# Gated linear attention and a GELU FFN on one core: one early table load, 112-row loads, halved copies in two units, and identity products in TensorE's waits

## The chip, the cores and the metric

The kernel runs on one core of a Trainium2 chip. The metric is the device time of one execution in microseconds. A core has five engines with a queue each, which run their instructions in the order of the program: TensorE (PE, with PEld for its weight loads), VectorE (DVE), ScalarE (ACT), GpSimd (POOL) and SyncE (SP, which here only issues transfers). A wait in one queue holds everything behind it.

## The reference, cut to what matters

```python
state = np.zeros((B, H, D, D))                 # B 4, H 8, S 768, D 48
for t in range(S):
    state = alpha[:, :, t, :, None] * state + np.einsum('bhd,bhe->bhde', k[:, :, t], v[:, :, t])
    y[:, :, t] = np.einsum('bhd,bhde->bhe', q[:, :, t], state)
x = y.transpose(0, 2, 1, 3).reshape(B * S, H * D)     # 3072 x 384
h = x @ w_in                                          # 384 x 2048
g = 0.5 * h * (1.0 + erf(h / sqrt(2)))
out = g @ w_out                                       # 2048 x 384
```

A recurrence with a decay per channel runs over 768 steps; its result is the input of a two-layer network with an exact GELU.

## The kernel before, in words

The sequence is cut into 12 groups g of 256 tokens, and each group into two units u of four heads: unit n = 2g + u. A unit is loaded as three tiles, alpha, keys and queries (`load_data`), two heads on partitions 0 to 47 and 64 to 111. Then VectorE scans alpha forward and backward (`ahead`, L254 and L263) and scales queries (L259) and keys (L268). TensorE makes the scores and turns the keys into one PSUM pair of banks (`scores`, `turned`, L283 and L291). ScalarE copies the turned keys out (kn, L301) and VectorE masks the scores (ss, L306); the two read the same two banks, and the program keeps them apart in time. TensorE makes the part inside a chunk and the states' increments (`inside`, L323 and L340), VectorE chains the states (`chain`, L358 and L360), TensorE adds the part from earlier chunks (`outside_part`, L384). The result is split into a high and a low part (x_high on ScalarE, L435, x_low on VectorE, L439). When both units of a group are there, `spread` (L448) moves 48-row pieces to their place by six small transfers, from the SP and the ACT queue in the first groups. Only then can the FFN of the group start.

The FFN's weights come in 16 pieces of 768 KB (`fetch`, L203, three buffers `st`). Each is turned into a high and a low part in four steps: top (ACT, L218), join (DVE, L222), high (ACT, L232), low (DVE, L235). Then `gemm1` (L456) multiplies x by w_in in three products, ScalarE makes the GELU twice (L522, L523), VectorE the low rest (L528), and `gemm2` (L540) multiplies by w_out. From group 4 on, two groups are taken together (L472, L490).

The order of instructions is set by a planner at build time: a list of operations with an engine, a cost from the table `COST`, the operations they wait for and a rank. It walks through time in steps of 0.05 and, whenever an engine is free, places the ready operation with the lowest rank; TensorE takes FFN steps when nothing of the recurrence is ready. The order that comes out is then written as it is into the engine's queues. A second thing that the planner does not see: each transfer uses one of eight semaphore lanes in turn, and the issue of a transfer waits until the one before on its lane has landed.

At the start 18 products of an identity matrix run on TensorE (L110) while the first data come in. After units 0 and 1 four range checks of alpha per group (`range_check`, L176, two per unit) are placed on ScalarE; the load of the unit that will use the same buffer waits for them.

Of the kernel before, what the change touches and what calls it, by code (L numbers as in the profile page):

```python
# [21 lines left out]
WARM = 18  # L22
# [15 lines left out]
def gla_then_gelu_ffn(ctx: ExitStack, tc: tile.TileContext, q, k, v, alpha, qg, kg, ag, vg, q0, k0, a0, w_in, w_out, out):  # L38
    nc = tc.nc
# [52 lines left out]
    y_first = first.tile([P, 2, BANK], F32, name="yfirst")  # L92
# [4 lines left out]
    def y_of(n):  # L97
        return y_first if n == 1 else ybank if n < SPLIT else sbank
# [203 lines left out]

    def masked(g, u):
        d = cur[g, u]
        d["ss"] = room(NU * g + u).tile([P, 2, NCH, CS], F32, tag="ss", bufs=1, name=f"ss_{g}_{u}")
        nc.vector.tensor_tensor(  # L306
            out=d["ss"],
            in0=d["s"][:, :, : 2 * C].rearrange("p h (c t) -> p h c t", t=CS),
            in1=mask.unsqueeze(1).unsqueeze(1).to_broadcast([P, 2, NCH, CS]),
            op=ALU.mult,  # L310
        )
# [390 lines left out]
    def plan_unit(n):  # L702
# [316 lines left out]
```

## Time and profile before

| what | value |
|---|---|
| median of 3 runs | 520.96 us (520.43 to 521.4) |
| the profiled execution | 520.84 us, of which its span is 519.0 us |
| TensorE busy | 489.8 us, 94% of the span |
| VectorE busy | 251.8 us, 49% |
| ScalarE busy | 200.4 us, 39% |
| moved by all transfers | 40.20 MB |

Times in the rows below are in microseconds from the start of the span unless marked ns. "Idle before" is time in which the engine had nothing to run, with what ended it. PEclk is the clock granted to TensorE as a share of 2.4 GHz: 1.00 is 2.4 GHz, 0.50 is 1.2 GHz.

### The profile page before, as it was taken

What the parts mean: (1) busy time and instruction counts of PE and PEld (TensorE: products, weight loads), DVE (VectorE), ACT (ScalarE), POOL (GpSimd) and SP (SyncE); (2) the same over time, 40 slices, a digit from 0 to 9 for tenths busy, and PEclk for the clock granted to TensorE, in tenths of its full rate; (3) what the DMA queues carried; (4) which work ended last, traced back from release to release, by engine and by line L of the source; (5) the groups of instructions that cost most, each with busy time, mean ns of one, the idle gap of its engine ahead of it and who ended that gap; (6) DMA issues with size and microseconds to landing.
All of it is one profiled execution on the core that took longest, in us unless ns stands there. A gap on an engine that the chain in (4) does not pass through costs nothing.

```text
span 519.0 us, 12171 instructions
## 1 busy us (share of the span) xinstructions
PE 489.8 (94%) x5190; PEld 418.8 (81%) x5190; DVE 251.8 (49%) x486; ACT 200.4 (39%) x386; POOL 31.3 (6%) x42
## 2 busy tenths in 40 slices
PE   5657999999999999999999999999999999999994
PEld 5556889899998999988888777788777788888883
DVE  4879977998888565121111558521433121211212
ACT  1647757445543342222222543232544222231311
POOL 2000001112211111000000101100000000000000
PEclk9569999999999999999999999999999999999998
DMA  8587757325541421000000332300100000100001
GB/s 317 176 268 230 239 145 231 92 58 159 139 129 43 140 80 46 1 30 1 1 1 1 107 92 56 85 1 0 63 18 3 14 1 0 62 0 1 0 1 67
DMA packets 24542, 40.20 MB, mean 77 GB/s; under 512 B 3872, under 2 KB 11616, under 8 KB 24480
## 3 DMA queue, kind: packets, MB, share of 16 engines
q1 hardware_dynamic: 22736, 34.06, 22.0%
q0 software_dynamic: 880, 3.93, 2.0%
q10 hardware_dynamic: 864, 1.34, 0.8%
q8 instruction: 43, 0.70, 0.6%
q14 instruction: 19, 0.16, 0.1%
HBM read 32.24 MB, written 4.72 MB: 71 GB/s over the span
## 4 chain that ended last, share of the span: by engine, by line
PE 82%; DVE 7%; ACT 4%; DMA 4%; issue 1%; SPq 0%; ACTq 0%; DVEq 0%
PE hw L472 26%; PE accw L490 17%; PE acc L540 10%; PE hp L456 9%; PE ybank L490 8%; DMA st<-in_moe_w_in_dram 2%; PE sbank L283 2%; PE sbank L291 2%; PE sbank L323 1%; PE sbank L384 1%; DMA ad<-in_ag_dram 1%; DVE st L222 1%; DVE pp L254 1%; ACT top L218 1%; PE ybank L323 1%
## 5 line engine op out<-in xcount | busy, mean ns | idle before, releaser
L528 DVE TENSOR_TENSOR glo<-hw,ghi 128x512 fp32r<-128x512 f32 x64 | 44.2, 691 | 172.3 <-ACT hw L523 172.3
L472 PE MATMUL hw<-x,wih 128*128 128x512 f32 x384 | 121.9, 398 | 0.0
L522 ACT ACTIVATE ghi<-hw 128x512 fp32r<-128x512 f32 x64 | 38.3, 598 | 177.7 <-PE hw L472 177.7
L472 PEld LDWEIGHTS hw<-x,wih 128*128 128x128 f32 x384 | 71.0, 188 | 16.1
L456 PE MATMUL hp<-x,wih 128*128 128x256 f32 x384 | 73.5, 291 | 7.6 <-DMA x<-z 7.5
L472 PE MATMUL hw<-x,wil 128*128 128x512 f32 x192 | 75.9, 395 | 0.0
L456 PEld LDWEIGHTS hp<-x,wih 128*128 128x128 f32 x384 | 60.9, 194 | 9.0 <-ACT top L218 7.7
L456 PE MATMUL hp<-x,wil 128*128 128x256 f32 x192 | 54.8, 286 | 0.0
L490 PE MATMUL accw<-ghi,woh 128*128 128x512 f32 x128 | 51.1, 399 | 0.0
L490 PE MATMUL accw<-ghi,wol 128*128 128x512 f32 x128 | 50.2, 393 | 0.0
L540 PE MATMUL acc<-woh,ghi 128*128 128x384 f32 x128 | 44.9, 351 | 0.0
L472 PEld LDWEIGHTS hw<-x,wil 128*128 128x128 f32 x192 | 36.0, 188 | 9.0
L540 PE MATMUL acc<-wol,ghi 128*128 128x384 f32 x128 | 43.0, 336 | 0.0
L490 PE MATMUL accw<-glo,woh 128*128 128x512 f32 x128 | 40.3, 391 | 0.0
L522 ACT ACTIVATE ghi<-hp 128x512 fp32r<-128x512 f32 x32 | 19.1, 598 | 52.3 <-PE hp L456 51.3
L523 ACT ACTIVATE hw<-hw 128x512 f32<-128x512 f32 x64 | 37.9, 592 | 0.0
L456 PEld LDWEIGHTS hp<-x,wil 128*128 128x128 f32 x192 | 37.3, 194 | 0.0
L263 DVE TENSOR_TENSOR_SCAN rp<-ad,rp,top 128x255 f32<-128x255 f32 x48 | 36.8, 809 | 0.1
L259 POOL TENSOR_TENSOR qd<-qd,pp 128x512 f32<-128x512 f32 x18 | 23.5, 1308 | 200.6 <-DMA st<-in_moe_w_in_dram 81.6
L528 DVE TENSOR_TENSOR glo<-hp,ghi 128x512 fp32r<-128x512 f32 x32 | 22.0, 686 | 22.3 <-ACT hp L523 22.1
L254 DVE TENSOR_TENSOR_SCAN pp<-ad,top 128x256 f32<-128x256 f32 x48 | 30.4, 675 | 4.9 <-DMA ad<-in_a_dram 4.9
L306 DVE TENSOR_TENSOR ss<-sbank,mask 128x512 f32<-128x512 f32 x23 | 15.9, 690 | 29.3 <-ACT kn L301 29.1
(105 smaller groups left out, 695.3 us busy)
## 6 DMA issues: line engine op xcount, KB each, us to landing
st<-in_moe_w_in_dram SPq DMA_DIRECT2D x8, 768.0 KB, 5.8
st<-in_moe_w_out_dram SPq DMA_DIRECT2D x8, 768.0 KB, 5.8
vn<-in_vg_dram SPq DMA_DIRECT2D x12, 384.0 KB, 5.1
ad<-in_ag_dram SPq DMA_DIRECT2D x40, 96.0 KB, 3.0
kd<-in_kg_dram SPq DMA_DIRECT2D x40, 96.0 KB, 2.3
qd<-in_qg_dram SPq DMA_DIRECT2D x40, 96.0 KB, 2.7
out_dram<-parts POOLq DMA_DIRECT2D x3, 768.0 KB, 3.6
x<-z SPq DMA_DIRECT2D x63, 32.0 KB, 2.0
```

Source lines behind the costliest of these rows:

```text
L254: nc.vector.tensor_tensor_scan(pp[:, i], at[:, i], top, MID, ALU.mult, ALU.min)
L259: (nc.vector if g < NSB else nc.gpsimd).tensor_tensor(out=qt, in0=qt, in1=pp, op=ALU.mult)
L263: nc.vector.tensor_tensor_scan(rp[:, i, G - 2 :: -1], at[:, i, G - 1 : 0 : -1], top[:, 1:], rp[:, i, G - 1 :], ALU.mult, ALU.min)
L283: nc.tensor.matmul(d["s"][o, h, t], lhsT=d["kt"][r, (2 * j + i) * CS : (2 * j + i + 1) * CS], rhs=d["qt"][r, i, t], start=True, stop=True)
L306: nc.vector.tensor_tensor(out=d["ss"], in0=d["s"][:, :, : 2 * C].rearrange("p h (c t) -> p h c t", t=CS), in1=mask.unsqueeze(1).unsqueeze( ...
L456: nc.tensor.matmul(hp[:, j, :], lhsT=a[:, j, i * P : (i + 1) * P], rhs=x[:, i, :], start=(i == 0 and n == 0), stop=(i == NK - 1 and n == 2),)
L472: nc.tensor.matmul(h, lhsT=a[:, j, i * P : (i + 1) * P], rhs=x[:, i, part], start=(i == 0 and n == 0), stop=(i == NK - 1 and n == 2),)
L490: nc.tensor.matmul(acc[i], lhsT=w[:, j, e], rhs=a, start=(f == 0 and k == 0 and w is wo_hi[f2]), stop=(f == NF - 1 and k == 1),)
L522: nc.scalar.activation(ghi, hp, AF.Gelu)
L523: nc.scalar.activation(hp, hp, AF.Gelu)
L528: nc.vector.tensor_tensor(out=glo, in0=hp, in1=ghi.bitcast(F32), op=ALU.subtract)
L540: nc.tensor.matmul(acc[t], lhsT=a[:, j, t * C : (t + 1) * C], rhs=w[:, j, :], start=(first and j == 0 and k == 0 and w is wo_hi[f]), stop= ...
```

## The change

ScalarE loads the table of the GELU as its first instruction (`preload_act_table`), ahead of its three transfer issues; the program then has one table load where it had two. All units are laid out with 64 rows for the first head, so that a load is one transfer of 112 rows (units 4 on) or 128 rows (the first four) where it was two of 48. In units 0 and 1 the copy of the keys and the mask are cut in two, one bank each, in opposite order. Unit 1 writes its result into `sbank` in place of a pair of banks of its own; that pair is now `spare_bank`, the target of the identity products, which nothing reads. Their number at the start is 22 where it was 18, and the planner places one more wherever, after its time 8.0 and before the first FFN step, TensorE has nothing ready for 0.33 (`turn`). The range checks of groups 0 and 1 wait until the spread of group 0 has landed, and the first step of weight pieces 0 and 1 waits for the copy of the keys of unit 0 and 1. Costs of a load and of the spread are set anew.

```diff
-WARM = 18
+WARM = 22
...
     def y_of(n):
-        return y_first if n == 1 else ybank if n < SPLIT else sbank
+        return sbank if n == 1 else ybank if n < SPLIT else sbank
...
-    warm = small_bank([P, P], "warm")
+    nc.scalar.preload_act_table(AF.Gelu)
+    def turn_over():
+        nc.tensor.matmul(spare_bank[:, 0, :P], lhsT=ident, rhs=ident, start=True, stop=True)
+
     for _ in range(WARM):
-        nc.tensor.matmul(warm, lhsT=ident, rhs=ident, start=True, stop=True)
+        turn_over()
...
-            if n < NB * NU:
-                eng = nc.scalar if n < NU and (i + u) % 2 else nc.sync
-                eng.dma_start(to, first[n])
-                continue
-            for h in range(2):
-                nc.sync.dma_start(to[h * DP : h * DP + D], src[g - NB, u, h])
+            rows = slice(0, P if n < NB * NU else DP + D)
+            eng = nc.scalar if n < NU and (i + u) % 2 else nc.sync
+            eng.dma_start(data[g % NB][name][rows, p].rearrange("p a t -> p (a t)"), src[n, rows])
...
-        nc.scalar.copy(d["kn"], d["s"][:, :, 2 * C : 4 * C])
+        for b in (slice(1, 2), slice(0, 1)) if NU * g + u < NU else (slice(0, 2),):
+            nc.scalar.copy(d["kn"][:, b], d["s"][:, b, 2 * C : 4 * C])
...
+        for b in (slice(0, 1), slice(1, 2)) if NU * g + u < NU else (slice(0, 2),):
+            nc.vector.tensor_tensor(
+                out=d["ss"][:, b],
...
+            if g == 1:
+                for o in (unit[u]["c%d" % side], d["c%d" % side]):
+                    o.deps.append(ready_x[0])
         if u == NU - 1:
             ready_x[g] = op("SP", "spread", lambda: spread(g), [d["xl"]], rank=-100, lands=3.2)
-            if g >= NSB:
-                ready_x[g].cost *= 2
+            ready_x[g].cost *= 2 if g >= NSB else 0.8
...
+    for n in range(NU):
+        wops[n]["u"].deps.append(unit[n]["kn"])
...
+        if 8.0 < t and not steps:
+            soon = [at for o in waiting["PE"] for at in [when(o)] if at is not None]
+            if not soon or min(soon) > t + COST["turn"]:
+                return Op("PE", "turn", turn_over)
```

What this makes of the queues is shown at three places. The first is TensorE from its start to the first FFN step; `hp_0` is the first FFN product, `sbank`, `sfirst`, `ybank` and `yfirst` are pairs of banks, `spare` is the pair that nobody reads. Before:

```order
L110 MATMUL sbank<-ident 128x128 x18
L283 MATMUL sbank<-qd_112,kd_111 64x64 x16
L291 MATMUL sbank<-ident,kd_111 128x128 x4
L323 MATMUL ybank<-ss_0_237,vn_109 64x64 x16
L340 MATMUL ybank<-vn_109,kn_0_235 64x48 x16
L283 MATMUL sfirst<-qd_112,kd_111 64x64 x16
L291 MATMUL sfirst<-ident,kd_111 128x128 x4
L384 MATMUL ybank<-qd_112,state_1_120 48x64 x4
...
L323 MATMUL yfirst<-ss_1_314,vn_109 64x64 x16
L340 MATMUL yfirst<-vn_109,kn_1_312 64x48 x16
L384 MATMUL yfirst<-qd_112,state_1_125 48x64 x4
```

And now:

```order
L111 MATMUL spare<-ident 128x128 x25
L283 MATMUL sbank<-qd_117,kd_116 64x64 x16
L291 MATMUL sbank<-ident,kd_116 128x128 x4
L111 MATMUL spare<-ident 128x128 x2
L325 MATMUL ybank<-ss_0_246,vn_114 64x64 x16
...
L325 MATMUL sbank<-ss_1_326,vn_114 64x64 x16
L342 MATMUL sbank<-vn_114,kn_1_323 64x48 x16
L111 MATMUL spare<-ident 128x128 x4
L386 MATMUL sbank<-qd_117,state_1_130 48x64 x4
...
L111 MATMUL spare<-ident 128x128 x19
L458 MATMUL hp_0_453<-x_369,wih_138 128x256 x2
```

25 identity products stand at the start, 2 after the scores of unit 0, 4 before the last step of unit 1 and 19 between it and the FFN. The order of the real work is unchanged here.

The second place is ScalarE up to the spread of group 0. Before:

```order
L165 DMA qd_112<-in_q_dram 128x512
L218 ACT_TABLE_LOAD
L218 CAST top_168<-st_182 128x768
L301 COPY kn_0_235<-sbank 128x512
...
L176 ACTIVATE junk_377,outside<-ad_110,hi_b 128x512
L435 CAST z_382<-yfirst 128x256
L435 CAST x_351<-yfirst 128x256
L176 ACTIVATE junk_392,outside<-ad_110,lo_b 128x512
L176 ACTIVATE junk_397,outside<-ad_110,hi_b 128x512
L448 DMA x_351<-z_382 16x512 x3
```

And now:

```order
L109 ACT_TABLE_LOAD
L168 DMA kd_116<-in_kg_dram 128x512
L168 DMA ad_115<-in_ag_dram 128x512
L168 DMA qd_117<-in_qg_dram 128x512
L302 COPY kn_0_243<-sbank 128x256 x2
L218 CAST top_173<-st_187 128x768
...
L437 CAST z_400<-sbank 128x256
L437 CAST x_369<-sbank 128x256
L232 CAST woh_154<-st_189 128x768
L450 DMA x_369<-z_400 16x512 x3
```

The table load moved ahead of the transfer issues, the first copy of keys ahead of the first weight step, and the range checks (`junk`) behind the spread.

The third place is SP around the spread of group 0; `ad`, `kd`, `qd` are a unit's alpha, keys and queries, `st` weight pieces. Before:

```order
L203 DMA st_380<-in_moe_w_out_dram 128x2x1536
L168 DMA ad_110<-in_ag_dram 48x512 x2
L168 DMA kd_111<-in_kg_dram 48x512 x2
L168 DMA qd_112<-in_qg_dram 48x512 x2
L448 DMA x_351<-z_382 16x512 x3
L203 DMA st_414<-in_moe_w_in_dram 128x2x1536
```

And now:

```order
L203 DMA st_397<-in_moe_w_out_dram 128x2x1536
L450 DMA x_369<-z_400 16x512 x3
L203 DMA st_426<-in_moe_w_in_dram 128x2x1536
L203 DMA st_437<-in_moe_w_out_dram 128x2x1536
L203 DMA st_509<-in_moe_w_in_dram 128x2x1536
L168 DMA ad_115<-in_ag_dram 112x512
L168 DMA kd_116<-in_kg_dram 112x512
L168 DMA qd_117<-in_qg_dram 112x512
L203 DMA st_596<-in_moe_w_out_dram 128x2x1536
```

The load of unit 4 moved from ahead of the spread to behind three more weight pieces; the eighth piece, st_596, now stands behind it.

## Rows read from the trace of the kernel before

**Rows 1.** Page, parts 1 and 2: the engines' busy time, and TensorE's granted clock in 40 slices of 13 us, in tenths.

```profile
PE 489.8 (94%) x5190; PEld 418.8 (81%) x5190; DVE 251.8 (49%) x486; ACT 200.4 (39%) x386; POOL 31.3 (6%) x42
...
PEclk9569999999999999999999999999999999999998
```

**Rows 2.** Busy time of each engine by stage: the stretch, its length, busy time and instructions of PE, PEld, DVE, ACT, POOL, then granted clock, share of the transfer engines, GB/s.

```profile
0.00:12.30 12.30, 7.41 (x72) 6.91 (x72) 6.29 (x13) 1.51 (x2) 2.86 (x17) 1.00 0.86 312
12.30:36.10 23.80, 11.95 (x234) 10.56 (x234) 20.18 (x39) 12.25 (x21) 0.00 (x0) 0.50 0.64 214
36.10:40.00 3.90, 3.45 (x55) 3.18 (x54) 1.25 (x2) 3.75 (x5) 0.00 (x0) 0.98 1.07 305
40.00:60.00 20.00, 16.51 (x301) 15.07 (x302) 19.46 (x37) 15.93 (x26) 0.00 (x0) 1.00 0.70 224
60.00:510.00 450.00, 448.62 (x4528) 381.84 (x4527) 203.24 (x395) 166.39 (x334) 28.40 (x25) 1.00 0.19 55
```

**Rows 3.** Waits in the first 60 us: who waited for whom, us in total, times, longest.

```profile
PE hp L456 <- DMA x<-z: 7.5, 1, 7.5
...
PE ybank L323 <- DVE ss L306: 5.4, 2, 3.9
```

**Rows 4.** Timeline of units 0 and 1: start, length, engine, line, operation, out<-in, count, and in brackets the idle time before it.

```profile
9.21 0.69 PE L283 MATMUL sbank<-qd,kd 48*64 48x64 f32 x32 [1.47 <-DVE kd L268]
...
9.83 0.66 PE L291 MATMUL sbank<-ident,kd 128*128 128x128 f32 x4
...
10.65 0.67 DVE L259 TENSOR_TENSOR qd<-qd,pp 128x512 f32<-128x512 f32 x1
...
10.77 1.28 ACT L218 ACT_TABLE_LOAD   x1 [10.77 <-DMA st<-in_moe_w_in_dram]
...
13.66 0.69 DVE L306 TENSOR_TENSOR ss<-sbank,mask 128x512 f32<-128x512 f32 x1 [2.33 <-ACT kn L301]
...
14.41 1.14 PE L323 MATMUL ybank<-ss,vn 64*64 64x64 f32 x32 [3.92 <-DVE ss L306]
...
16.43 1.13 PE L283 MATMUL sfirst<-qd,kd 48*64 48x64 f32 x32
...
17.49 1.11 PE L291 MATMUL sfirst<-ident,kd 128*128 128x128 f32 x4
...
20.01 1.13 PE L323 MATMUL yfirst<-ss,vn 64*64 64x64 f32 x32 [0.58 <-DVE ss L306]
...
22.66 0.84 DVE L360 TENSOR_TENSOR state<-yfirst,state 128x96 f32<-128x96 f32 x3
...
23.55 0.89 PE L384 MATMUL yfirst<-qd,state 48*48 48x64 f32 x24 [1.59 <-DVE state L360]
```

**Rows 5.** The same view from the end of unit 1 to the first FFN steps.

```profile
24.84 0.35 ACT L435 CAST z<-yfirst 128x256 fp32r<-128x256 f32 x1
...
25.49 0.42 DVE L439 TENSOR_TENSOR z<-yfirst,z 128x256 fp32r<-128x256 f32 x1
25.83 0.42 DVE L439 TENSOR_TENSOR x<-yfirst,x 128x256 fp32r<-128x256 f32 x1
...
29.49 2.07 SPq L448 DMA_DIRECT2D x<-z  x3
...
31.96 0.77 PE L456 MATMUL hp<-x,wih 128*128 128x256 f32 x2 [7.51 <-DMA x<-z]
...
36.07 0.74 PE L283 MATMUL sbank<-qd,kd 48*64 48x64 f32 x32
...
37.30 1.28 ACT L522 ACT_TABLE_LOAD   x1
...
38.59 0.60 ACT L522 ACTIVATE ghi<-hp 128x512 fp32r<-128x512 f32 x1
...
41.05 0.69 PE L323 MATMUL ybank<-ss,vn 64*64 64x64 f32 x32 [1.50 <-DVE ss L306]
```

**Rows 6.** VectorE's groups in the first 60 us: line, engine, operation, names, shapes, count, then busy time and the mean of one in ns, then idle time before.

```profile
L222 DVE SCALAR_TENSOR_TENSOR st<-st,top 128x768 int32<-128x768 int32 x10 | 9.5, 955 | 2.1 <-ACT top L218 2.1
L254 DVE TENSOR_TENSOR_SCAN pp<-ad,top 128x256 f32<-128x256 f32 x10 | 6.3, 676 | 4.9 <-DMA ad<-in_a_dram 4.9
L263 DVE TENSOR_TENSOR_SCAN rp<-ad,rp,top 128x255 f32<-128x255 f32 x8 | 5.5, 733 | 0.0
L235 DVE TENSOR_TENSOR wil<-st,wih 128x768 fp32r<-128x768 f32 x5 | 4.7, 944 | 0.0
```

**Rows 7.** Three stretches of 1 us, columns as in rows 2.

```profile
3.00:4.00 1.00, 1.00 (x7) 1.00 (x6) 0.00 (x0) 0.00 (x0) 0.62 (x3) 1.00 1.02 361
6.00:7.00 1.00, 1.00 (x11) 1.00 (x10) 0.93 (x4) 0.00 (x0) 0.00 (x0) 1.00 1.04 380
...
36.00:37.00 1.00, 1.00 (x35) 0.86 (x35) 0.03 (x1) 0.78 (x1) 0.00 (x0) 0.89 1.04 424
```

**Rows 8.** Transfers: what the SP queue waited for in the first 100 us (first row), the issue of the eighth weight piece (second), and issues with KB each and median us from issue to landing (the rest).

```profile
SPq L448 <- DMA ad<-in_ag_dram: 2.1, 2, 1.8
...
44.04 0.39 SPq L203 DMA_DIRECT2D st<-in_moe_w_out_dram  x1
...
x<-z SPq DMA_DIRECT2D x63, 32.0 KB, 2.0
...
x<-z ACTq DMA_DIRECT2D x9, 32.0 KB, 4.2
```

More of the change, by code (lines that the diff above doesn't have):

```diff
@@ L28 @@
 COST = dict(
+    turn=0.33,
     scan=1.7, back=1.45, times=0.71, q=1.35, scores=1.2, kn=0.6, mask=0.62, inside=1.2, chain=1.15, outer=0.7, carry=0.26,
@@ L37, in gla_then_gelu_ffn @@
 @with_exitstack
-def gla_then_gelu_ffn(ctx: ExitStack, tc: tile.TileContext, q, k, v, alpha, qg, kg, ag, vg, q0, k0, a0, w_in, w_out, out):
+def gla_then_gelu_ffn(ctx: ExitStack, tc: tile.TileContext, q, k, v, alpha, qg, kg, ag, vg, w_in, w_out, out):
     nc = tc.nc
@@ L91, in gla_then_gelu_ffn @@
     s_first = first.tile([P, 2, BANK], F32, name="sfirst")
-    y_first = first.tile([P, 2, BANK], F32, name="yfirst")
+    spare_bank = first.tile([P, 2, BANK], F32, name="spare")
     def s_of(n):
@@ L305, in masked @@
         d["ss"] = room(NU * g + u).tile([P, 2, NCH, CS], F32, tag="ss", bufs=1, name=f"ss_{g}_{u}")
[L306 to L311, printed above, removed]
+        for b in (slice(0, 1), slice(1, 2)) if NU * g + u < NU else (slice(0, 2),):
+            nc.vector.tensor_tensor(
+                out=d["ss"][:, b],
+                in0=d["s"][:, b, : 2 * C].rearrange("p h (c t) -> p h c t", t=CS),
+                in1=mask.unsqueeze(1).unsqueeze(1).to_broadcast([P, b.stop - b.start, NCH, CS]),
+                op=ALU.mult,
+            )
     def inside(g, u):
@@ L714, in plan_unit @@
         sp, yp, rp = (next((unit[m] for m in range(n - 1, -1, -1) if of(m) is of(n)), {}) for of in (s_of, y_of, room))
-        d["load"] = op("SP", "load", lambda: load_data(g, u), [old.get(x) for x in ("outer", "scores", "inside", "c0", "c1")], rank=r - 30, lands=2.0, kb=786 if old == {} else 590)
-        d["load"].cost = 0.9 if n < NU else 1.4 if old == {} else 2.6
+        d["load"] = op("SP", "load", lambda: load_data(g, u), [old.get(x) for x in ("outer", "scores", "inside", "c0", "c1")], rank=r - 30, lands=2.0, kb=786 if old == {} else 688)
+        d["load"].cost = 0.9 if n < NU else 1.4
         if u == NU - 1:
@@ L724, in plan_unit @@
         shared = [yp.get("xh"), yp.get("xl")] if y_of(n) is s_of(n) else []
+        if n == NU:
+            shared = [unit[1]["xh"], unit[1]["xl"]]
         d["scores"] = op("PE", "scores", lambda: (scores(g, u), turned(g, u)), [d["keys"], d["q"], sp.get("mask"), sp.get("kn"), *shared], rank=r)
@@ L727, in plan_unit @@
         d["mask"] = op("DVE", "mask", lambda: masked(g, u), [d["scores"], rp.get("inside")], rank=-1)
-        d["inside"] = op("PE", "inside", lambda: inside(g, u), [d["mask"], d["kn"], yp.get("xh"), yp.get("xl")], rank=r)
+        d["inside"] = op("PE", "inside", lambda: inside(g, u), [d["mask"], d["kn"], yp.get("xh"), yp.get("xl"), *([unit[0]["mask"], unit[0]["kn"]] if n == 1 else [])], rank=r)
         d["chain"] = op("DVE", "chain", lambda: chain(g, u), [d["inside"], pp_.get("carry")], rank=-1)
@@ L962, in spare @@
     def spare(x, value):
-        x = x[:2].reshape(4, 2, D, 512)
-        return _np.concatenate((x, _np.full((4, 2, 64 - D, 512), value, x.dtype)), axis=2).reshape(4, P, 512)
-    qg, kg, ag = grouped(q), grouped(k), grouped(alpha)
-    kg = kg.reshape(-1, H // 4, 2, D, 2, 4, 64).swapaxes(4, 5).reshape(ag.shape)
+        x = grouped(x).reshape(-1, 2, D, 512)
+        return _np.concatenate((x, _np.full((len(x), 2, 64 - D, 512), value, x.dtype)), axis=2).reshape(-1, P, 512)
     w_in = _np.concatenate((main, rest), axis=2).reshape(NK, P, DFF // P, P)
@@ L973, in _laid_out @@
         "alpha": alpha.swapaxes(2, 3),
-        "qg": qg[2:],
-        "kg": kg[2:],
-        "ag": ag[2:],
+        "qg": spare(q, 0.0),
+        "kg": spare(k, 0.0).reshape(-1, P, 2, 4, 64).swapaxes(2, 3).reshape(-1, P, 512),
+        "ag": spare(alpha, 1.0),
         "vg": v.reshape(B, H // 4, 2, 2, S // 256, 4, 64, D)
```

6 lines of the change are left out of this document (1 added, 5 removed).

## The prediction

> **What bounds the kernel now.** I read the stages first. TensorE is busy 489.8 of 519.0 us [rows 1], but not evenly. From 60 to 510 us it waits 450 - 448.62 = 1.4 us in all, so that stage is TensorE's own work, which the change leaves alone [rows 2]. What can be won lies ahead of it. TensorE stands still 12.30 - 7.41 = 4.9 us in the first 12.3 us, 23.80 - 11.95 = 11.9 us from 12.3 to 36.1, 0.45 us up to 40 and 3.5 us from there to 60. From 12.3 to 36.1 its clock is 0.50, the 1.2 GHz level; it is back at 1.00 by 40 [rows 2]. The slices of the page show the same dip and no other before the tail [rows 1].
>
> The waits say why [rows 3]. The longest is 7.5 us before the first FFN step, ended by the transfers x<-z, the spread. Next come 5.4 us before `inside`, ended by VectorE's mask, which itself waits for ScalarE's copy, 2.33 us in unit 0 [rows 4]. So the bound up to 32 us is one chain: unit 0, unit 1, spread, first FFN step. VectorE runs along it with little slack: idle 23.80 - 20.18 = 3.6 us from 12.3 to 36.1, 2.65 us from 36.1 to 40, and only 0.5 us of the 20 us to 60 [rows 2]. Whatever comes sooner must also find VectorE free.
>
> **The change part by part.** I follow that chain through the new queues with durations of the old rows; negative is sooner.
>
> *Start.* Identity products: at the low rate 7 records in 1 us, later 11 [rows 7]. A product is two records, so 0.29 or 0.18 us. The 18 of before end at about 7.7, where the 1.47 us wait before 9.21 begins [rows 4]; seven more at 0.18 end at 9.0, just ahead of the scores at 9.21. Cost 0. The table load, 1.28 us [rows 4], now delays three issues on ScalarE's queue by that much. The keys of unit 0 are among them, needed shortly before 9.21; the first alpha on SP meanwhile shares the transfer engines with less. Not shown in the trace: between +1.3 (the whole delay reaches the scores) and -1.3 (the first scan starts that much earlier). I take 0, since the engines move the same bytes in total.
>
> *Unit 0.* Before, the copy stood behind the table load and a weight step, and the mask came at 13.66, 3.2 us after the scores ended at 9.83 + 0.66 = 10.49 [rows 4]. Now the copy stands first, and the mask can start when VectorE ends qd at 10.65 + 0.67 = 11.3. A half costs about 0.35 on ScalarE and 0.42 on VectorE, the prices of 128x256 operations at 24.84 and 25.49 [rows 5]. Two halves side by side are 0.84 at most, against 1.26 in a row. So `inside` starts at about 12.2 in place of 14.41: -2.2.
>
> *Unit 1.* Mask end 12.1, backward scans 2 x 0.73 [rows 6], keys at the mask's price of 0.69 [rows 4]: scores at 14.3 in place of 16.43. They took 18.60 - 16.43 = 2.17 at 1.2 GHz, against 1.28 at 2.4 GHz in unit 0 [rows 4]. At the high clock they end at 15.6. VectorE's chain of about 1.1 (three of its four steps take 0.84 [rows 4]) and one join of 0.95 [rows 6] come first, then the mask: `inside` at 17.2 in place of 20.01, -2.8. Here VectorE's new order puts the scan of unit 2 (2 x 0.68 [rows 6], and an estimated 0.3 for two small operations), a low part (0.69, a full-size operation like the mask) and a carry (0.28, as a chain step) ahead of the second chain; these 2.6 us hide what the clock gives in `inside`. Second chain 19.7 to 20.8, last step of unit 1 at 20.9 in place of 23.55 [rows 4]: -2.65.
>
> *Spread.* On VectorE follow 0.94 + 0.95 [rows 6], a carry of 0.28 and the low part's 0.76 (25.49 to 26.25 [rows 5]): it ends at 23.7 in place of 25.83 + 0.42 = 26.25 [rows 5]. Before, TensorE started 5.7 us after that, because six loads stood ahead on SP and a lane made the spread wait for one of them [rows 8]; SP issued at 29.49 to 31.56. Those loads are now behind, and the lanes ahead hold transfers of the opening. One issue is 0.7, landing 2.0 on SP and 4.2 on ScalarE's queue, which had the contention [rows 8]. From 23.7 that is 26.4 to 28.6; I take 27.0, near the lower end, because one weight piece still shares the engines. The first FFN step moves from 31.96 to 27.0: -5.0. The 19 products end at 21.4 + 19 x 0.18 = 24.8, or at 27.4 with 0.29 and a last step at the low rate: cost 0 to 0.4.
>
> *Behind it.* At 1.2 GHz the first FFN step and the next scores' start lie 36.07 - 31.96 = 4.1 us apart [rows 5]. Now VectorE decides when those scores start: 23.7 plus two joins (0.95 each), two low parts (0.94 each), qd (0.67), backward scans (1.46) and keys (0.69) is 30.3, with 0.6 that I allow for ScalarE's casts 30.9. That is -5.2 against 36.07. To unit 2's `inside` come 1.6 (scan), 0.94, 0.69 and 0.69, and 0.4 for a GELU that follows a late weight step: 35.2 against 41.05, -5.8. The second table load, 1.28 us at 37.30 [rows 5], falls away inside this.
>
> *The rest.* In 22 of 24 units copy and mask are as before, TensorE's real work is the same, and the one issue per load in place of two empties SP, which nobody waits for. 112 rows move 17% more bytes than 96; from 40 to 60 us the engines are 70% busy [rows 2], which hides it. If not, 96 KB more per unit at the 224 GB/s of that stage is 0.4 us for a unit, and four units load there: 0 to 1.7.
>
> Sum: TensorE's work shifts by -5.2 (unit 2's scores) to -5.8 (its `inside`); the range of the start (1.3 either way) and the bytes (up to 1.7) lie around it. I take -5.5. From the profiled execution, 520.84, that is 515.3; the median of before is 0.12 higher, so 515.4.
>
> A rule speaks against the early table load being so cheap. The row has the load from 10.77 to 12.05, and a GELU at 38.59 directly behind the second, 1.29 after its start [rows 4, 5]. The Trainium skill, "ScalarE: Activation LUTs", section "What ACT_TABLE_LOAD costs", counts a drain of about 1.38 us on top, 2.66 in all. By it the start's upper bound would be +2.7, and the sum with all of that on the path -2.8, where the rows' 1.28 makes it -4.2; the rows show no such drain.
>
> **The rivals.**
>
> *The clock falls all the same.* In the old run it read 1.00 until about 12.3, after TensorE stopped at 10.49, and came back near 36.1, after it had taken up the FFN at 31.96 [rows 2, 4, 5, 7]. The new queue has 2 and 4 products where the gaps on my chain are 1.8 us and about 2.2, so TensorE rests in part of both. Then unit 1's scores cost 0.9 more, its last step 0.35, and the first FFN step up to 2.0 more. The queue of VectorE hides most of it: about +1.2 at unit 2's scores, 516.5. The Trainium skill, "TensorE: Matmul & The Clock Gate", section "What's actually happening", says that "the default state is throttled, and activity releases the throttle"; the old run agrees, with 0.50 through a stage half idle (11.95 of 23.80).
>
> *The gain is given back between 40 and 60.* VectorE is 97% busy there [rows 2]. If weight pieces or VectorE, not the FFN's start, set the pace up to 60, then what TensorE wins before becomes waiting after. VectorE's idle time from 12.3 to 40 is 3.6 + 2.65 = 6.2 us; were only a third of it usable, the gain is 2.1: 518.7. Against it: most of that idle is waiting that this chain causes.
>
> *Slower.* The load of unit 4 waits for the second range check of unit 0, which now stands behind the spread among weight steps, and the eighth weight piece is behind that load on SP. My chain has that check at about 36 and the piece issued at 37.5, where it was 44.04 [rows 8]. Every us that ScalarE makes the check later than 38.5 holds the last nine pieces by one. From 44.0 on the kernel is slower than before; a check at 45.5 gives 522. For it: ScalarE is 15.93 of 20 us busy from 40 to 60 [rows 2]. Against it: it must fall 8 us behind.
>
> *It does not do what it says.* If the copies still follow each other and the spread still waits on a lane, the chain keeps its length: 520.8.
>
> **How the numbers follow.** Forecast 0.50 (its own range 513.3 to 517), clock falls 0.18, given back 0.19, slower 0.08, nothing 0.05. What a measurement here can tell from no change is about 0.2%, 1 us. Faster by more: 0.50 + 0.18 and most of 0.19, 0.83. Same: nothing and a little of given back, 0.08. Slower: 0.09. The range goes from 512.8, where waits between 40 and 60 also shrink, to 520.2, up to the edge of no change.
>
> **What would show it.** In the new profile: `inside` of unit 0 near 12.2 and of unit 1 near 17.2; the first L458 row near 27; unit 2's scores near 31; granted clock 1.00 from 12 to 36, where the first rival shows 0.50; one table load; 60 to 510 still almost without waits. Wrong if VectorE's row from 40 to 60 turns into waits for weight pieces, or if SP stands long before the first 112-row load.

## The result, and the profile after

| | before | after |
|---|---|---|
| median of 6 runs each | 520.94 us | 524.4 us (522.51 to 526.36) |
| ratio | | 1.0069, 95% interval 1.005 to 1.0089 |
| the profiled execution | 520.84 us, span 519.0 | 523.48 us, span 521.8 |

The change makes the kernel slower by 0.7%. The forecast was 515.4 us, and its range ended at 520.2: it was wrong in size and in sign. Yet the opening went as forecast, or better.

Page of after, parts 1 and 2: the lines that answer to [rows 1].

```profile
PE 495.3 (95%) x5254; PEld 423.3 (81%) x5254; DVE 252.7 (48%) x488; ACT 199.6 (38%) x387; POOL 31.0 (6%) x42
...
PEclk9999799999999999999999999999999999999998
```

Stages of after, columns as in [rows 2], with two stretches more (40 to 80 and 55 to 63).

```profile
0.00:12.30 12.30, 9.87 (x128) 9.36 (x132) 7.66 (x17) 3.00 (x4) 2.86 (x17) 1.00 0.85 311
12.30:36.10 23.80, 18.58 (x380) 16.81 (x370) 22.45 (x44) 14.54 (x24) 0.00 (x0) 1.00 0.74 249
36.10:40.00 3.90, 2.62 (x44) 2.22 (x43) 3.78 (x9) 3.87 (x8) 0.00 (x0) 1.00 0.71 223
40.00:60.00 20.00, 13.91 (x197) 12.75 (x196) 15.19 (x29) 11.36 (x20) 0.00 (x0) 0.90 0.90 274
60.00:510.00 450.00, 446.03 (x4509) 379.01 (x4508) 201.53 (x391) 165.20 (x331) 28.18 (x25) 1.00 0.19 56
...
40.00:80.00 40.00, 32.47 (x525) 29.53 (x524) 30.95 (x59) 24.65 (x45) 0.00 (x0) 0.91 0.68 206
55.00:63.00 8.00, 5.82 (x48) 5.25 (x48) 5.84 (x13) 5.71 (x10) 0.00 (x0) 0.57 0.62 207
```

The stretches up to 40, from 40 to 80 and behind 80 us before, and then the first and the last of them after:

```profile
0.00:40.00 40.00, 22.81 (x356) 20.65 (x356) 27.73 (x54) 17.52 (x27) 2.86 (x17) 0.70 0.75 253
40.00:80.00 40.00, 36.39 (x641) 32.92 (x642) 36.43 (x67) 28.26 (x47) 0.00 (x0) 1.00 0.63 193
80.00:510.00 430.00, 428.73 (x4189) 364.00 (x4188) 186.27 (x364) 154.06 (x313) 28.40 (x25) 1.00 0.17 50
...
0.00:40.00 40.00, 31.07 (x534) 28.39 (x535) 33.89 (x67) 21.41 (x35) 2.86 (x17) 1.00 0.77 266
80.00:510.00 430.00, 427.47 (x4181) 362.22 (x4180) 185.78 (x362) 151.92 (x305) 28.18 (x25) 1.00 0.17 52
```

Read the two kernels together. The old dip of the clock from 12 to 36 us is gone in this execution. A new one stands at 55 to 63 (0.57). From 40 to 80 TensorE stands still 40 - 32.47 = 7.5 us where it stood 3.6, and VectorE, whose 97% the prediction built on, is now idle 4.8 of 20 us from 40 to 60.

Rows picked from the timeline of the opening after, answering to [rows 4, 5].

```profile
0.94 1.28 ACT L109 ACT_TABLE_LOAD   x1 [0.94 <-PEq L1010]
0.97 0.39 ACTq L168 DMA_DIRECT2D kd<-in_kg_dram  x1
4.13 1.28 DVE L254 TENSOR_TENSOR_SCAN pp<-ad,top 128x256 f32<-128x256 f32 x2 [4.13 <-DMA ad<-in_ag_dram]
8.88 0.69 PE L283 MATMUL sbank<-qd,kd 48*64 48x64 f32 x32
10.94 0.76 DVE L308 TENSOR_TENSOR ss<-sbank,mask 128x256 f32<-128x256 f32 x2 [0.33 <-ACT kn L302]
11.42 0.96 PE L325 MATMUL ybank<-ss,vn 64*64 64x64 f32 x29 [0.81 <-DVE ss L308]
13.78 0.69 PE L283 MATMUL sfirst<-qd,kd 48*64 48x64 f32 x32 [0.88 <-DVE kd L268]
16.25 1.28 PE L325 MATMUL sbank<-ss,vn 64*64 64x64 f32 x32 [0.71 <-DVE ss L308]
19.96 0.55 PE L386 MATMUL sbank<-qd,state 48*48 48x64 f32 x24 [0.89 <-DVE state L362]
22.17 2.17 SPq L450 DMA_DIRECT2D x<-z  x3
26.57 0.48 PE L458 MATMUL hp<-x,wih 128*128 128x256 f32 x2 [1.62 <-DMA x<-z]
28.89 0.69 PE L283 MATMUL sbank<-qd,kd 48*64 48x64 f32 x32
32.63 0.69 PE L325 MATMUL ybank<-ss,vn 64*64 64x64 f32 x32 [0.32 <-DVE ss L308]
```

| step | before | forecast | after |
|---|---|---|---|
| `inside` of unit 0 | 14.41 | 12.2 | 11.42 |
| scores of unit 1 | 16.43 | 14.3 | 13.78 |
| `inside` of unit 1 | 20.01 | 17.2 | 16.25 |
| last step of unit 1 | 23.55 | 20.9 | 19.96 |
| first FFN step | 31.96 | 27.0 | 26.57 |
| scores of unit 2 | 36.07 | 30.9 | 28.89 |
| `inside` of unit 2 | 41.05 | 35.2 | 32.63 |

At 33 us the new kernel is 8.4 us ahead. What happens to the lead is read from the timeline of after from 43 to 65 us. The rows picked are first steps of weight pieces on ScalarE (L218), and what waits behind them.

```profile
43.26 1.07 ACT L218 CAST top<-st 128x768 f16<-128x768 bf16 x1 [2.33 <-DMA st<-in_moe_w_out_dram]
45.68 0.59 ACT L524 ACTIVATE ghi<-hp 128x512 fp32r<-128x512 f32 x1
46.33 0.44 PE L542 MATMUL acc<-woh,ghi 128*128 128x384 f32 x1 [1.75 <-ACT ghi L524]
47.70 1.07 ACT L218 CAST top<-st 128x768 f16<-128x768 bf16 x1 [0.94 <-DMA st<-in_moe_w_in_dram]
48.63 0.57 ACT L302 COPY kn<-sbank 128x512 f32<-128x512 f32 x1
49.23 0.69 DVE L308 TENSOR_TENSOR ss<-sbank,mask 128x512 f32<-128x512 f32 x1 [1.73 <-ACT kn L302]
49.98 0.69 PE L325 MATMUL ybank<-ss,vn 64*64 64x64 f32 x32 [1.30 <-DVE ss L308]
55.62 1.05 ACT L218 CAST top<-st 128x768 f16<-128x768 bf16 x1 [2.15 <-DMA st<-in_moe_w_out_dram]
57.18 0.69 PE L542 MATMUL acc<-woh,ghi 128*128 128x384 f32 x1 [2.28 <-ACT ghi L524]
62.39 0.83 PE L291 MATMUL sbank<-ident,kd 128*128 128x128 f32 x4
63.32 0.57 ACT L302 COPY kn<-sbank 128x512 f32<-128x512 f32 x1
64.66 0.69 PE L325 MATMUL ybank<-ss,vn 64*64 64x64 f32 x32 [1.44 <-DVE ss L308]
```

ScalarE stands at the eighth piece, which has not landed (2.33 us); the GELU is behind it, and TensorE waits for the GELU (1.75). It stands at the ninth (0.94); the key copy is behind it, then VectorE's mask, then TensorE (1.30). It stands at the tenth (2.15), again with a GELU behind it, and TensorE waits 2.28. The last wait, 1.44 before 64.66, has no piece in it: the key copy of unit 4 starts at 63.32, as soon as the turned keys are there (62.39 and 0.83 more), the mask follows, and TensorE has no FFN product in its order for that time. The pieces land late. From 20 to 70 us the median from issue to landing is 5.9 and 7.1 us (4.7 and 4.8 in the kernel before); the plan reckons 786 thousand bytes at 330 GB/s and 2.2 us more, 4.6 where nothing is ahead of the piece. The tenth is late for another reason: its step starts 4.8 us after its issue at 50.86, and the issue had waited for a buffer.

```profile
st<-in_moe_w_out_dram SPq DMA_DIRECT2D x5, 768.0 KB, 5.9
st<-in_moe_w_in_dram SPq DMA_DIRECT2D x5, 768.0 KB, 7.1
```

### The profile page after: what moved, and what is told of

Read it like the earlier page. It is cut to its first block, busy times and chain, and to the rows that moved or that the text cites. A ratio compares the mean times of both kernels' runs of the same rounds, so it can differ in the third digit from the quotient of the medians.

```text
span 521.8 us, 12212 instructions
## 1 busy us (share of the span) xinstructions
PE 495.3 (95%) x5254; PEld 423.3 (81%) x5254; DVE 252.7 (48%) x488; ACT 199.6 (38%) x387; POOL 31.0 (6%) x42
## 4 chain that ended last, share of the span: by engine, by line
PE 81%; DVE 3%; DMA 1%; ACT 1%; issue 1%
PE hw L474 26%; PE accw L492 17%; PE hp L458 10%; PE acc L542 9%; PE ybank L492 8%; PE sbank L283 2%; PE sbank L291 2%; DMA st<-in_moe_w_out_dram 1%; PE sbank L325 1%; PE sbank L386 1%; PE sbank L342 1%; DVE rp L263 1%; PE ybank L386 1%; PE ybank L325 1%; DVE pp L254 0%
## 5 line engine op out<-in xcount | busy, mean ns | idle before, releaser
L458 PE MATMUL hp<-x,wih 128*128 128x256 f32 x384 | 71.8, 287 | 1.6 <-DMA x<-z 1.6
L458 PEld LDWEIGHTS hp<-x,wih 128*128 128x128 f32 x384 | 59.5, 190 | 2.8 <-issue 1.8
L308 DVE TENSOR_TENSOR ss<-sbank,mask 128x512 f32<-128x512 f32 (+1 forms) x24 | 15.9, 668 | 30.7 <-ACT kn L302 29.0
```

The source lines that it names most:

```text
L308: nc.vector.tensor_tensor(out=d["ss"][:, b], in0=d["s"][:, b, : 2 * C].rearrange("p h (c t) -> p h c t", t=CS), in1=mask.unsqueeze(1).unsq ...
L458: nc.tensor.matmul(hp[:, j, :], lhsT=a[:, j, i * P : (i + 1) * P], rhs=x[:, i, :], start=(i == 0 and n == 0), stop=(i == NK - 1 and n == 2),)
```

## The experiments

Every ratio is against the kernel before, on the same chip. Three theories stood at first: the loads that now follow weight pieces collide with them (A), 112 rows move too many bytes (B), or the weights set the pace whatever the order (C). After the first four runs a fourth was added: the plan, made for pieces that land early, puts steps that need a piece ahead of work that does not (D). "Landing number" is the 2.2 in `plan_piece`; it moves no transfer by itself, only the order that the planner makes.

**1. The range checks free again**, in the changed kernel.

```diff
-            if g == 1:
-                for o in (unit[u]["c%d" % side], d["c%d" % side]):
-                    o.deps.append(ready_x[0])
```

> The changed kernel without the rule that holds the range checks of groups 0 and 1 behind the first spread; all else kept, so the loads of units 4 and 5 can stand early on SP again. Theory A (those loads, moved among the weight pieces, delay the pieces and TensorE waits for them from 45 to 65 us): 516 to 519 us, the ninth and tenth weight piece issued before 47 us, and waits of TensorE from 45 to 65 of under 3 us. Theory B (the 17% more bytes of the 112-row loads are what fills the transfer engines): 523 to 525, as the changed kernel. Theory C (the weights set the pace up to 60 us whatever the order, so an earlier start is always given back): 520 to 522.

522.59 us, 1.0042 (1.0025 to 1.0059), between the ranges of B and C and far from A's. By the medians the late checks are 1.8 us of the loss in this plan; the two intervals overlap a little.

**2. Two transfers of 48 rows** in place of one of 112, the order as it is.

```diff
-            eng.dma_start(data[g % NB][name][rows, p].rearrange("p a t -> p (a t)"), src[n, rows])
...
+            for h in range(2):
+                eng.dma_start(to[h * DP : h * DP + D], src[n, h * DP : h * DP + D])
```

> The changed kernel with each load of unit 4 on issued as two transfers of 48 rows, as before; every queue keeps its order, the bytes are those of before. Theory A (place of the loads): 522 to 525, the same waits from 45 to 65. Theory B (bytes): 518 to 521, with the weight pieces issued at 37 to 40 us landing within 6 us where they took 6.1 and 8.6. Theory C: 522 to 525.

525.08 us, 1.0079 (1.0056 to 1.0102): the bytes are not it, B falls.

**3. Identity products left out of the program**, those that the planner places; all else in its place.

```diff
-                return Op("PE", "turn", turn_over)
+                return Op("PE", "turn", lambda: None)
```

> The changed kernel without the 25 identity products after the first scores (2, 4 and 19) and the 3 that the planner adds at the start; the planner still leaves their places, so all other queues are the same. If the products hold the clock and the clock sets the opening: granted clock 0.50 in part of 12 to 30 us, unit 2's scores 1 to 3 us later than 28.9, and 524 to 527 in the end. If the end is set by weight pieces (theories A to C): unit 2's scores later but the total within 1 us of the changed kernel, 523 to 525.

523.58 us, 1.0048 (1.0029 to 1.0066). The clock falls to 0.64 from 12 to 36 us, and the end does not move by more than its own uncertainty. Stage of this kernel:

```profile
12.30:36.10 23.80, 15.37 (x337) 13.71 (x338) 21.77 (x43) 13.40 (x23) 0.00 (x0) 0.64 0.73 231
```

**4. The rule for the range checks alone**, put into the kernel before (the three lines of experiment 1, added).

> The kernel before with one part of the change alone: range checks of groups 0 and 1 wait for the first spread. Theory A: loads of units 4 to 6 fall among the weight pieces here too; the spread comes sooner, the pieces later: 521 to 525, with new waits of TensorE between 45 and 65. Theories B and C: 519 to 521, since bytes and weights are as before.

528.62 us, 1.0149 (1.0126 to 1.0172), above every range expected. One added rule in the plan costs 7.8 us. The longest wait of TensorE in this kernel from 40 to 66 us:

```profile
PE acc L540 <- ACT ghi L522: 5.3, 1, 5.3
```

The GELU stands behind a weight step that waits 5.2 us for its piece: the reading of after, larger. That piece, the tenth, was issued at 56.48, behind the loads of unit 6 on SP; in the kernel before it was issued at 51.55, ahead of them.

**5. Landing number 4.0**, in the changed kernel.

```diff
-        d["get"] = op("SP", "fetch", lambda: fetch(n), [q3.get("lo")], rank=r - 30.5, lands=2.2, kb=786)
+        d["get"] = op("SP", "fetch", lambda: fetch(n), [q3.get("lo")], rank=r - 30.5, lands=4.0, kb=786)
```

> The changed kernel with one number of the planner altered: a weight piece is taken to land 1.8 us later than it thought (4.0 for 2.2 behind the last byte), near the 6 to 8 us that the changed kernel's page shows from issue to landing. Only the order of the queues changes. Theory D (pieces land later than the plan believes, and ScalarE's first weight step, which waits for one, holds the key copy and the GELU behind it): 514 to 519, ScalarE's waits for pieces from 40 to 65 under 4 us. Theory C (weights set the pace whatever the order): 521 to 524.

517.09 us, 0.9933 (0.9919 to 0.9947): 7.3 us less than the changed kernel by order alone, and faster than both. Timeline of this kernel:

```profile
41.75 0.58 ACT L302 COPY kn<-sbank 128x512 f32<-128x512 f32 x1
...
43.45 0.69 PE L325 MATMUL ybank<-ss,vn 64*64 64x64 f32 x32
43.78 1.08 ACT L218 CAST top<-st 128x768 f16<-128x768 bf16 x1 [0.75 <-DMA st<-in_moe_w_out_dram]
...
46.98 0.60 ACT L524 ACTIVATE ghi<-hp 128x512 fp32r<-128x512 f32 x1 [0.67 <-PE hp L458]
...
49.84 1.07 ACT L218 CAST top<-st 128x768 f16<-128x768 bf16 x1 [1.77 <-DMA st<-in_moe_w_in_dram]
...
52.27 1.79 SPq L450 DMA_DIRECT2D x<-z  x3
...
56.38 1.13 PE L283 MATMUL sbank<-qd,kd 48*64 48x64 f32 x32 [3.49 <-DVE kd L268]
```

Key copy and GELU now stand ahead of the weight steps that wait. `inside` of unit 3 starts at 43.45 (49.98 in after), the spread of group 1 at 52.27 (58.70). C falls.

**6. Loads of units 4 to 7 cut to 16 rows** of 112 (the rest of their data is left out and stays old).

```diff
-            rows = slice(0, P if n < NB * NU else DP + D)
+            rows = slice(0, P if n < NB * NU else 16 if n < 8 else DP + D)
```

> The changed kernel with the loads of units 4 to 7 cut to 16 of 112 rows, so that these units compute on stale rows; every queue keeps its order. It leaves out 0.58 MB for each of four units. Theory A (these loads collide with the pieces on the transfer engines): 516 to 520, the pieces issued at 37 and 39 us land within 5 us where they took 6.1 and 8.6. Theory D without collision: 522 to 525, the pieces land as late as before.

524.08 us, 1.0072 (1.0044 to 1.0099): A falls as the cause of the loss. Part of the collision is there. Without those bytes the median from issue to landing is 4.7 us for both kinds of pieces (20 to 70 us), where it was 5.9 and 7.1; the eighth lands in 4.7 us (6.1), the ninth still takes 7.9 (8.6). In the same order, most pieces land sooner and the time does not move. D had expected its time with pieces as late as before, and they were not.

**7 and 8. Pieces 6 to 11 fetched by half** (the second half of their weights is left out), in the changed kernel and in the kernel before.

```diff
+    slots = [stage.tile([P, 8 * DM + 4], U16, tag=f"st{i}", bufs=1, name=f"st{i}") for i in range(STAGE)]
...
-        staged[n] = stage.tile([P, 8 * DM + 4], U16, tag="st", name=f"st_{n}")
+        staged[n] = slots[n % STAGE]
...
-            staged[n][:, SHIFT : 8 * DM + SHIFT].rearrange("p (two e) -> p two e", two=2), pieces[n][0].bitcast(U16)
+            staged[n][:, SHIFT : 8 * DM + SHIFT].rearrange("p (two e) -> p two e", two=2)[:, : 1 if 6 <= n <= 11 else 2],
+            pieces[n][0].bitcast(U16)[:, : 1 if 6 <= n <= 11 else 2],
```

> The changed kernel with weight pieces 6 to 11 (counted from 0) fetched by half, the other half left as it was in the buffer; every queue keeps its order. Theory D (late pieces are the whole of what is given back): 512 to 517, since the opening's gain of 5 to 7 us then stays. Theory C with VectorE or ScalarE as the pace: 520 to 523, although the pieces come sooner.

> The kernel before with the same half pieces 6 to 11. It gives the level that the halved pieces reach without the change. Theory D: 519 to 521, as before, since its waits for pieces are small (4.4 us on ScalarE, none on TensorE's chain after 60). Theory C: 516 to 519.

522.37 us, 1.0026 (1.0007 to 1.0045), and 519.42 us, 0.998 (0.9969 to 0.9991). Half the bytes give 2.0 us, and 1.1 in the kernel before (520.55 beside it). D had expected 512 to 517 in the changed kernel, and C 520 to 523. So D misses here, although the half pieces land sooner than the plan's 4.6 (changed kernel, 20 to 70 us):

```profile
st<-in_moe_w_in_dram SPq DMA_DIRECT2D x3, 384.0 KB, 4.2
st<-in_moe_w_out_dram SPq DMA_DIRECT2D x3, 384.0 KB, 3.4
```

The order stays, and a piece still waits for its buffer: the tenth is issued at 50.67 where it was 50.86.

**9 to 12. The landing number further**: with the checks free as well; in the kernel before; at 5.5; and at 4.0 with the identity products left out as in experiment 3.

> The changed kernel with two edits at once: the planner takes 4.0 us in place of 2.2 for the landing of a weight piece, and the range checks of groups 0 and 1 no longer wait for the spread. If the landing number and the late checks are two separate losses, they add: 517.1 less the 1.8 us that the checks gave alone, about 515.3, which is the forecast of the blind prediction. If both only repair one thing, the order of ScalarE's queue between 40 and 60 us, the second adds nothing: 516.5 to 518. If the checks in the way of the GELU cost more than their wait, it may even be slower, 519 or more.

> The kernel before with the one number alone: 4.0 us in place of 2.2 for the landing of a weight piece. If the later landing keeps the opening's gain, and the kernel before had no such loss, the time stays near 520.9 (within 1.5 us). If the number is a gain of its own that has nothing to do with the change, it falls by as much as in the changed kernel, to 514 to 516. If the number fits one plan by chance only, it may rise to 523 or more.

> The changed kernel with 5.5 us in place of 2.2 for the landing of a weight piece (4.0 gave 517.1). If the plan is better the nearer it is to what a piece takes in this kernel (6.2 and 7.7 us from issue to landing in the middle, of which the planner's own transfer time is about 2.4), the time is 515.5 to 517.5. If 4.0 was a lucky order, 5.5 gives anything up to the 524 of the changed kernel.

> The changed kernel with 4.0 us for the landing of a weight piece, and with the identity products that the planner places left out of the program (the 22 at the start stay; the order of everything else is as with 4.0). If the clock of the opening decides nothing even where the order keeps the gain, 517 as with the products, within 1 us. If the gain of the products only shows once the order keeps it, the opening's lower clock costs 1.5 to 3 us: 518.5 to 520.

| kernel | us | ratio |
|---|---|---|
| changed, 4.0, checks free | 517.54 | 0.9943 (0.9929 to 0.9958) |
| before, 4.0 | 520.8 | 1.0 (0.9988 to 1.0013) |
| changed, 5.5 | 516.89 | 0.9923 (0.9892 to 0.9954) |
| changed, 4.0, no planned products | 519.06 | 0.9965 (0.9952 to 0.9977) |

With experiment 5, three different orders of the changed kernel come out within 0.7 us of each other, so 4.0 was no lucky draw in this kernel; the checks add nothing on top of it; and in the kernel before the same number changes nothing in sum. There, by the estimate used below, TensorE is 3.0 us further at 40 us and loses 2.5 more from 40 to 80, so a later landing number is no gain by itself. The products, worth nothing that can be told from noise in experiment 3, are worth 1.7 us (by the ratios) to 2.0 (by the medians) here. How is not shown: by the same estimate the lead at 40 us is 6.1 us with and without them.

**13 and 14. ScalarE's order alone.** The landing number moves everything at once. Here three weight steps are moved in the finished plan of the changed kernel (13), or two are put back ahead in the plan with 4.0 (14: the first step of the eighth piece ahead of the key copy of unit 3, of the ninth ahead of the third GELU). `behind(a, b)` puts a, and what depends on it, directly behind b in the order that is written out; the edit of 13:

```diff
+    behind(wops[7]["u"], steps[2]["gelu"])
+    behind(wops[8]["u"], unit[3]["kn"])
+    behind(wops[9]["u"], unit[3]["xh"])
```

> The changed kernel with its own plan, in which three operations alone are moved on ScalarE once the plan is made: the first step of the eighth weight piece goes behind the third GELU (its join on VectorE goes behind one scan with it), that of the ninth behind the key copy of unit 3, that of the tenth behind the high part of unit 3. Loads, pieces, TensorE's order stay. If the order of ScalarE's queue between 40 and 60 us is the cause, the key copy of unit 3 comes about 3 us earlier than 48.6, TensorE's waits for the GELU (4.0 us in all) shrink to under 1, and the time falls to 518 to 521. If what the landing number changed elsewhere (the loads on SP, VectorE's order) was the cause, the time stays at 523 to 525.

> The changed kernel with 4.0 us for the landing of a weight piece (517.1), in which two operations alone are moved back on ScalarE: the first step of the eighth weight piece ahead of the key copy of unit 3, that of the ninth ahead of the third GELU. If the order of ScalarE's queue is the cause, the key copy then waits about 3 us for the eighth piece and the GELU about 4 us for the ninth, and the time rises to 520 to 523. If it is not, it stays within 1 us of 517.

525.07 us, 1.008 (1.0052 to 1.0109), and 517.43 us, 0.994 (0.9921 to 0.9959). D in this narrow form falls: ScalarE's order by itself neither brings the gain nor takes it. In 13 the fourth FFN step ends at 57.2 (61.4 in after), but the wait comes back one step further on:

```profile
60.30 1.13 PE L283 MATMUL sbank<-qd,kd 48*64 48x64 f32 x32 [3.09 <-DVE kd L268]
65.16 1.13 PE L325 MATMUL ybank<-ss,vn 64*64 64x64 f32 x32 [2.68 <-DVE ss L308]
```

VectorE's join of the tenth piece (L222) stands ahead of unit 4's keys, and waits for the same late piece.

**15 and 16. VectorE's too.** The steps of the tenth to twelfth piece also go behind unit 4's keys and key copy (15); these alone (16).

```diff
+    behind(wops[9]["u"], ready_x[1])
+    behind(wops[9]["c1"], unit[4]["keys"])
+    behind(wops[10]["u"], unit[4]["kn"])
+    behind(wops[9]["hi"], unit[4]["kn"])
+    behind(wops[11]["u"], wops[10]["u"])
```

> The changed kernel with its own plan, in which steps of five weight pieces are moved behind the recurrence on both engines: on ScalarE the first step of the eighth behind the third GELU, of the ninth behind the key copy of unit 3, of the tenth behind the spread of group 1, of the eleventh and twelfth behind the key copy of unit 4; on VectorE the join of the tenth behind the keys of unit 4, and its high part on ScalarE behind the key copy of unit 4. Loads, pieces and TensorE's order stay. If late pieces hold the recurrence through both queues up to 65 us, as the trace of the run before reads (3.1 us before the scores of unit 4, 2.7 before its part inside a chunk), the scores of unit 4 come near 57.6 where they came at 60.3, its part inside a chunk near 60.5 where it came at 65.2, and the time falls by 3 to 5 us, to 519.5 to 522. If it is the loads or the order of TensorE that the landing number repaired, the lead is lost again behind 65 us and the time stays at 523 to 525.

> As the run with all five pieces moved, but the eighth and ninth stay where the plan has them; only the tenth to twelfth move. If the later of the waits (55 to 65 us) is the one that sets the time, this gives all of the gain: 519.5 to 522. If the earlier ones matter too, it gives about half, 521.5 to 523.5; if neither does, 524 as the changed kernel.

523.68 us, 1.0046 (1.0024 to 1.0069), and 523.8 us, 1.0059 (1.0038 to 1.0081). Unit 4's scores come at 57.46, as expected, and the wait moves on to the mask (kernel 15):

```profile
57.46 0.70 PE L283 MATMUL sbank<-qd,kd 48*64 48x64 f32 x32 [0.28 <-DVE kd L268]
...
62.94 1.13 PE L325 MATMUL ybank<-ss,vn 64*64 64x64 f32 x32 [4.20 <-DVE ss L308]
```

**17 and 18. TensorE's order.** A product step for that wait, and the mask ahead of VectorE's scan and join, on top of 15 (17); the product step alone in the changed kernel (18).

```diff
+    behind(unit[4]["inside"], steps[4]["gemm1"])
+    behind(wops[9]["c1"], unit[4]["mask"])
+    behind(unit[5]["scan"], unit[4]["mask"])
```

> As the run with all five weight pieces moved behind (523.7), and besides on TensorE the first product step of the fifth FFN step stands ahead of unit 4's part inside a chunk where it stood behind it, and on VectorE the mask of unit 4 stands ahead of the scan of unit 5 and of the join of the tenth piece. In the run before TensorE waited 4.2 us between the scores of unit 4 (57.5) and its part inside a chunk (62.9) with nothing in its order that could run, and its clock fell. If TensorE's own order is what gave the lead away there, that wait shrinks to under 1, the part inside a chunk comes near 61, and the time falls by 3 to 5 us to 518.5 to 520.5. If the lead is lost for another reason (weights that come too late for the steps behind 65 us), it stays within 1.5 us of 523.7.

> The changed kernel with its own plan and one thing moved: on TensorE the first product step of the fifth FFN step stands ahead of unit 4's part inside a chunk. If TensorE's order is the larger part by itself, 521 to 522.5; if it helps only when the recurrence comes sooner on the other engines too, 523 to 524.5, as the changed kernel.

523.95 us, 1.0057 (1.0036 to 1.0077), and 524.67 us, 1.007 (1.0048 to 1.0092). The wait moves on once more, to the chain of states behind the low part of the tenth piece:

```profile
62.09 0.69 PE L325 MATMUL ybank<-ss,vn 64*64 64x64 f32 x32
...
67.79 1.10 PE L386 MATMUL ybank<-qd,state 48*48 48x64 f32 x32 [4.67 <-DVE state L362]
```

**What the runs add up to.** TensorE's loss from 40 to 80 us, worked out as its idle time plus its busy time times what the mean clock lacks of 1 (an estimate: the mean of such a stretch is coarse):

| kernel | idle | clock | loss | span |
|---|---|---|---|---|
| before | 3.6 | 1.00 | 3.6 | 519.0 |
| after | 7.5 | 0.91 | 10.5 | 521.8 |
| 13: ScalarE's steps behind | 8.9 | 0.87 | 12.9 | 523.5 |
| 15: VectorE's too | 7.0 | 0.91 | 9.9 | 522.1 |
| 17: TensorE's too | 8.0 | 0.91 | 10.9 | 522.4 |
| landing number 4.0 | 4.4 | 0.91 | 7.6 | 516.6 |
| 14: 4.0, two steps back ahead | 4.5 | 0.91 | 7.7 | 516.8 |
| landing number 5.5 | 5.1 | 0.96 | 6.5 | 515.5 |
| 4.0 and checks free | 4.1 | 1.00 | 4.1 | 515.7 |
| before, landing number 4.0 | 4.7 | 0.96 | 6.1 | 519.3 |

```profile
40.00:80.00 40.00, 34.88 (x549) 32.05 (x548) 34.16 (x64) 27.11 (x49) 1.31 (x1) 0.96 0.86 246
```

(the row of 5.5). Moved by hand, link by link, the loss stays near 10 to 13; planned anew with a later landing number, it falls to 4 to 8. From 80 to 500 us TensorE waits 2.5 us in after, and 0.4 with 4.0 or 5.5. So the runs show that the order of the queues behind 40 us, as a whole, gives the lead away: other orders of the same instructions and the same bytes keep it. They do not show that late pieces are why the first order is bad, which is D in its wide form. In the old order half pieces, which land sooner than the plan has them, bring 2.0 us of the 7.3 (experiment 7), sooner pieces in experiment 6 nothing, and with 5.5, the fastest, the pieces land in 6.7 and 7.1 us, as late as in after. Which of the moves in the new plan suffice was not found either: those tried in the old plan gave nothing that can be told from noise. The version that beats both kernels is the change with 4.0 or 5.5.

## Why the prediction was wrong

*Start, Unit 0, Unit 1* were right in mechanism, and a little short. The first scan starts at 4.13, not 4.9 [rows 6]: the table load, 0.94 to 2.22, did not hold back the three issues on ScalarE's queue (the first at 0.97). The bound of +1.3 was not touched. The scores started at 8.88, behind the 25 products, although their keys were ready at about 8.4: the sum had the end of the products nearly right (9.0), and their cost, put at 0, about half a microsecond too low. The Trainium skill, "ScalarE: Activation LUTs", section "What ACT_TABLE_LOAD costs", counts a drain of about 1.38 us on top of a load; this trace shows none on the chain.

*Spread* was right: 26.57 for 27.0. *Behind it* came sooner still than forecast (-8.4 for -5.8 at unit 2's `inside`).

The rival on the clock was wrong for the opening of this execution, where the clock read 1.00, and came true elsewhere: 0.57 from 55 to 63, with waits of TensorE of 1.75, 1.30, 0.76 and 2.28 us between 44 and 57. That the opening kept its clock was in part luck: in kernels with the same order on TensorE, ScalarE and VectorE up to 40 us the profiled executions read 1.00 (2, 13, 15, 16, 18), 0.93 (17) and 0.86 (6, 7) from 12 to 36 us. The Trainium skill, "TensorE: Matmul & The Clock Gate", section "What's actually happening", says that activity releases the throttle; the trace agrees, before at 12 to 36 us and now at 55 to 63.

The step that failed is the sum, with *The rest*: "TensorE's work shifts by -5.2 (unit 2's scores) to -5.8 (its `inside`)", and "TensorE's real work is the same". A lead at unit 2 was taken for a lead at the end. The lead itself was as large as the sum had it. Behind 40 us TensorE still has 489.8 - 22.8 = 467.0 us of work before, and after it has 495.3 - 31.1 = 464.2, of which the low clock accounts for 2.9: 461.3, or 5.7 less (an estimate from busy times). That is less than the 8.4 us at unit 2's `inside`, since TensorE waits another 2.0 us in after up to 40 and before it was only waiting from 40 to 41.05.

Then the lead is lost. Between 40 and 80 us TensorE's loss rose from 3.6 to 10.5, 6.9 us more; from 80 to 510 its waits rose from 1.3 to 2.5; 0.3 is left for the end. That makes the 2.8 us by which the span grew. The prediction had read VectorE's 97% from 40 to 60 as work that moves along. It was work of an order that fitted: the new plan, in which every time ahead of it had moved, interleaved weight steps with the recurrence anew, and that order made TensorE wait. Why this order is worse than those with the later landing number stays open.

*The gain is given back between 40 and 60* named the place, and at 518.7 left a third of VectorE's idle time as gain; more than all of it went. The *Slower* rival was right that the range checks can cost time, and had another path: it needed the eighth piece issued after 44.0, and it was issued at 37.18, near the 37.5 of the forecast. What the rule for the checks costs, 7.8 us on the kernel before (experiment 4), comes, as its trace reads, mostly through a weight step ahead of a GELU. The prediction weighed only pieces held on SP behind the loads; that path has its part there, with the tenth piece issued at 56.48, but the rest of the way, from a piece through ScalarE to TensorE, was not in its account.

The wrong signs it had named were the right ones to look for: from 60 to 510 us TensorE waits 4.0 us where it was 1.4, and VectorE's stretch from 40 to 60 turned into waits behind pieces.

## What to carry to other kernels

Where a planner writes in-order queues, a change early in the program is a new order everywhere behind it; a lead read at one point is a gain only if the waits behind that point are read too, in the new order with measured transfer times. Vary what such a planner assumes of landing times: one number moved this kernel by 7.3 us, while it moved the kernel before by nothing. Late transfers seen ahead of a wait are not yet its cause: with pieces that landed sooner than planned, in the same order, only 2.0 of the 7.3 us came back. And in a chain of in-order queues a wait taken out at one link shows up at the next; here a new plan repaired the loss, and five sets of moves by hand did not.

## What was not expected of the hardware

A table load that runs on ScalarE (0.94 to 2.22) did not delay transfers issued from ScalarE's queue behind it (0.97). A 768 KB piece of w_in landed in a median of 7.1 us where it took 4.8 in the kernel before, and the one issued at 39.12 was waited for until 47.70, 8.6 us, in a stretch where the transfer engines' share was 0.90 (40 to 60 us). With the loads of four units cut to 16 of 112 rows the median was 4.7 again (experiment 6). And TensorE's clock from 12 to 36 us read between 0.86 and 1.00 in executions of kernels with the same order up to there.
